# Second expert layers: one ScalarE function, h tanh(softplus(h)), used twice in place of sigmoid, square, reciprocal and products

## The chip, the core and the metric

The kernel runs on one core of a Trainium2 chip. The metric is device time in microseconds (us), the median of several executions. A core has five engines that run their own instruction queues in order and meet only through semaphores: TensorE (PE, with its weight loads shown as PEld), VectorE (DVE), ScalarE (ACT), GpSimd (POOL) and SyncE (SP), which issues the DMA transfers.

## What is computed

Attention over 4 batches, 8 heads and 576 tokens, in which only scores within tau of a row's maximum count, feeds two expert layers, each with 2304 tokens, width 512 and hidden width 2048. The change lies in the second:

```python
def _moe2_ref(x, w_in, w_out) -> np.ndarray:
    h = x @ w_in
    sp = np.where(h > 20.0, h, np.log1p(np.exp(np.minimum(h, 20.0))))
    g = h * np.tanh(sp)
    return (g @ w_out).astype(np.float32)
```

So between the two products of the second layer each element of h becomes g = h tanh(softplus(h)). With d = sigmoid(h) and t = (d - 1)^2 this is h (1 - t) / (1 + t), which is what the kernel before works out.

## The kernel before, in words

Every product is made from two-part operands: a value is split into a high part in TensorE's reduced 32-bit format (fp32r) and a low part, the rest. A product takes three terms: high by high, low by high and high by low.

The program has three stages: attention together with the first expert layer for the first three batches, the first layer for the last batch (while the weights of the second layer are split), and the second layer, `moe2`, which is the stage of this study. The weights arrive as `wraw`, are scaled by ACT (L64), put together in `wa` by DVE (L66 to L68, three instructions), and split into high part (ACT, L71) and low part (POOL, L72). The last quarters of the second product's weights, `w2o` in the rows, are still being split when `moe2` begins; the generator `rest` puts those steps between the stage's own.

`moe2` works on five blocks of tokens, four of 512 columns and one (number 4, the fourth in order) of 256. A block has 16 hidden chunks `fc` of 128 rows, 80 pairs (block, chunk) in all. For each pair:

- `hidden`: 12 matmuls make the chunk of h in PSUM. Even chunks use the pool `hp`, odd ones `mm` (named `hm`), with two buffers each, so chunk i + 4 needs the buffer of chunk i back.
- `act1`, `act2`, `act3` and `low`: the function. ACT makes the sigmoid d from h (L505) and the square t (L506). POOL makes -1 - t in d (L510). DVE makes (t - 1) h in t, which is the last reader of h (L511), and the reciprocal of d (L512). POOL multiplies t and d (L516), ACT copies the high part g2h (L519), POOL subtracts it to get the low part g2l (L523).
- `output`: 12 matmuls (6 in the block of 256 columns) add the chunk's part to the output sums o_0 to o_3, eight or four with g2h first, then those with g2l.

Code order is given by the loop at the end of `moe2`: in step i come `hidden` of chunk i, the functions, and `output` of chunk i - LAG, with LAG = 3. `act3` works on the chunk of the step before. The order of instructions in each engine's queue is then set by a scheduler, which may move them from code order. After chunk 15 the sums are copied to `os` by ACT (L548) and DVE (L546), and SP stores them (L552).

The tags `gh` and `gl` of the pool `gp` have six buffers each; d and g2h are allocated from the first, t and g2l from the second.

Of the kernel before, what the change touches and what calls it, by code (L numbers as in the profile page):

```python
# [8 lines left out]
F32 = mybir.dt.float32  # L9
F32R = mybir.dt.float32r  # L10
I32 = mybir.dt.int32
AF = mybir.ActivationFunctionType
ALU = mybir.AluOpType
PSUM = bass.MemoryType.PSUM

P = 128
# [3 lines left out]
class Fused:  # L20
# [12 lines left out]
    def consts(self, pool):  # L33
        nc = self.nc
        i2 = pool.tile([P, 192], F32, name="ident")
        self.ident, self.swap = i2[:, 0:128], i2[:, 64:192]
        make_identity(nc, self.ident)
        nc.gpsimd.tensor_copy(i2[:, 128:192], i2[:, 0:64])
        self.tau_c = pool.tile([P, 1], F32, name="tau_c")
        self.s_c = pool.tile([P, 1], F32, name="s_c")  # L40
        self.b_c = pool.tile([P, 1], F32, name="b_c")
        self.neg1 = pool.tile([P, 1], F32, name="neg1")
        nc.gpsimd.memset(self.neg1, -1.0)
        self.colsum = pool.tile([P, 4], F32, name="colsum")
        self.cb = pool.tile([P, 4], F32, name="cb")

# [279 lines left out]
    def attention(self):  # L326
# [4 lines left out]
        N = 9 * self.B * self.NP  # L331
        LAG = 7
        for n in "kq":
# [8 lines left out]
        tes = {}  # L342
        for k in range(N + LAG + 2):
            pr, ti = divmod(k, 9)
# [12 lines left out]
            elif fin:  # L357
                fin()
                fin = None
            j = k - LAG  # L360
            if 0 <= j < N:
# [109 lines left out]
    def moe2(self, rest):  # L471
        nc = self.nc
        blocks = (0, 1, 2, 4, 3)
        work = [(bi, fc) for bi in blocks for fc in range(16)]
        ys, hps, gs, outs = {}, {}, {}, {}

        def load(bi):
            n = 512 if bi < 4 else 256
            ys[bi] = [], [], n
            for e in range(4):  # L480
                for i, tag in enumerate(("xh", "xl")):
                    t = self.xp.tile([P, n], F32R, tag=tag, name=f"y2{bi}_{e}_{i}")
                    nc.sync.dma_start(t.bitcast(F32), self.yT[bi, e, i] if bi < 4 else self.yrem[e, i])
                    ys[bi][i].append(t)

        def hidden(bi, fc):
            yh, yl, n = ys[bi]
            w = self.w2["i", fc // 4]
            fs = slice((fc % 4) * 128, (fc % 4) * 128 + 128)
            hp = self.mm.tile([P, 512], F32, tag="mm", name=f"hm{bi}_{fc}") if fc % 2 else \  # L490
                self.hp.tile([P, 512], F32, tag="hp", name=f"hp{bi}_{fc}")
            i = 0
            for kc in range(4):
                for wl, yy in ((0, yh), (0, yl), (1, yh)):
                    nc.tensor.matmul(hp[:, :n], w[:, wl, kc, fs], yy[kc], start=(i == 0), stop=(i == 11))  # L495
                    i += 1
            hps[bi, fc] = hp[:, :n]

        def act1(bi, fc):

            h = hps.pop((bi, fc))
            n = ys[bi][2]
            d = self.gp.tile([P, n], F32, tag="gh", name=f"d{bi}_{fc}")
            t = self.gp.tile([P, n], F32, tag="gl", name=f"t{bi}_{fc}")
            nc.scalar.activation(d, h, AF.Sigmoid)  # L505
            nc.scalar.activation(t, d, AF.Square, bias=self.neg1)  # L506
            return h, d, t

        def act2(bi, fc, h, d, t):
            nc.gpsimd.tensor_scalar(d, t, -1.0, -1.0, op0=ALU.mult, op1=ALU.add)  # L510
            nc.vector.scalar_tensor_tensor(t, t, 1.0, h, op0=ALU.subtract, op1=ALU.mult)  # L511
            nc.vector.reciprocal(d, d)  # L512

        def act3(bi, fc, h, d, t):
            n = ys[bi][2]
            nc.gpsimd.tensor_tensor(t, t, d, op=ALU.mult)  # L516
            gh = self.gp.tile([P, n], F32R, tag="gh", name=f"g2h{bi}_{fc}")
            gl = self.gp.tile([P, n], F32R, tag="gl", name=f"g2l{bi}_{fc}")
            nc.scalar.copy(gh, t)  # L519
            gs[bi, fc] = (gh, gl)  # L520

            def low():
                nc.gpsimd.tensor_tensor(gl, t, gh.bitcast(F32), op=ALU.subtract)  # L523

            return low

        def output(bi, fc):
            gh, gl = gs.pop((bi, fc))
            n = ys[bi][2]
            w = self.w2["o", fc // 4]  # L530
            terms = [(gh, 0), (gh, 1), (gl, 0)]
            todo = [(i, t) for i in range(3) for t in range(n // 128)]
            if fc == 15:
                todo.sort(key=lambda it: it[1])
            for i, t in todo:
                if fc == 0 and i == 0:
                    outs[t] = self.op.tile([P, 512], F32, tag=f"o{t}", name=f"o{bi}_{t}")
                g, wl = terms[i]
                nc.tensor.matmul(outs[t], g[:, t * 128:t * 128 + 128], w[:, wl, fc % 4, :],  # L539
                                 start=(fc == 0 and i == 0), stop=(fc == 15 and i == 2))  # L540
            if fc < 15:
                return
            for t in range(n // 128):
                o = self.yp.tile([P, 512], F32, tag=f"y{t}", name=f"os{bi}_{t}")
                if t % 2:
                    nc.vector.tensor_copy(o, outs[t])  # L546
                else:
                    nc.scalar.copy(o, outs[t])  # L548
                if bi < 4:

                    dst = self.out[bi * 576:bi * 576 + 512, :].rearrange("(j c) e -> c j e", c=4)[t]
                    nc.sync.dma_start(dst, o)  # L552
                else:
                    for i in range(2):
                        r0 = (2 * t + i) * 576 + 512
                        nc.sync.dma_start(self.out[r0:r0 + 64, :], o[64 * i:64 * i + 64, :])

        LAG = 3
        load(0)
        prev = None  # L560
        n = len(work)
        for i in range(n + LAG):
            if i < n:
                bi, fc = work[i]
                if fc == 11 and bi != blocks[-1]:
                    load(blocks[blocks.index(bi) + 1])
                hidden(bi, fc)
                cur = (bi, fc) + act1(bi, fc)
            else:
                cur = None  # L570
            low = act3(*prev) if prev else None
            if cur:
                act2(*cur)
            if low:
                low()
            prev = cur
            if i >= LAG:
                output(*work[i - LAG])
            for _ in range(2):
                next(rest, None)  # L580
            yield 5200
# [136 lines left out]
```

## Time and profile before

| | |
|---|---|
| median of 3 runs | 1219.41 us (1215.17 to 1219.55) |
| the profiled execution | 1216.89 us |
| its span, first to last instruction | 1215.1 us |
| `moe2`, first matmul to last (start times of the trace) | 792.69 to 1208.46 us |
| busy over the span: PE, DVE, ACT, POOL | 95%, 71%, 49%, 54% |
| mean granted TensorE clock | 0.984 of full |

The profiled execution is 1.8 us longer than its span and lies 2.5 us under the median. Each engine's busy share is an average over stages that have different limits, so what follows is read from `moe2` alone. A matmul in the trace has a modelled end, after which the next has long begun: for the pace of TensorE the start times count, not the durations.

### The profile page before, as it was taken

The page shows a single profiled execution, that of the slowest core. Times are in us where ns is not written, and L with a number is a line of the kernel's source. Part 1 is how long each engine was busy: PE and PEld are TensorE (multiplying, and loading weights), DVE is VectorE, ACT ScalarE, POOL GpSimd, SP SyncE. Part 2 cuts the span into 40 slices and gives each one's busy share as a digit, 9 for nine tenths or more (in the row PEclk, how much of TensorE's full clock was granted, in tenths as well). Part 3 has the DMA queues.
Part 4 walks back from the last instruction along what each step waited for, and adds up shares of the span by engine and source line. Part 5 has one row for each costly group of instructions (what it writes and reads, how often), then busy time and mean ns, then how long its engine had stood idle before and what let it go on. Part 6 is the DMA issues. An engine that isn't in the chain of part 4 may idle for free.

```text
span 1215.1 us, 20290 instructions
## 1 busy us (share of the span) xinstructions
PE 1153.1 (95%) x7104; PEld 983.9 (81%) x7104; DVE 868.4 (71%) x1585; ACT 592.5 (49%) x1153; POOL 657.9 (54%) x841
## 2 busy tenths in 40 slices
PE   5888999999899999999999999988999999999998
PEld 4666878877788998988998999966888888888886
DVE  5888777878885465664652799799977676767865
ACT  4666666575555544455532575453433333344332
POOL 5566777786644343335431354346755655555654
PEclk8989999999999999999999999989999999999999
DMA  5556466576585445474433898842130020020000
GB/s 129 157 142 180 111 210 183 168 208 175 175 288 165 144 144 165 127 227 132 131 99 111 288 323 267 293 148 70 36 104 1 1 70 1 8 97 1 18 1 35
DMA packets 123671, 161.88 MB, mean 133 GB/s; under 512 B 57392, under 2 KB 78896, under 8 KB 123568
## 3 DMA queue, kind: packets, MB, share of 16 engines
q1 hardware_dynamic: 123568, 160.58, 43.2%
q8 instruction: 56, 0.92, 0.3%
q14 instruction: 47, 0.39, 0.1%
HBM read 107.48 MB, written 30.93 MB: 114 GB/s over the span
## 4 chain that ended last, share of the span: by engine, by line
PE 59%; DVE 13%; DMA 10%; POOL 6%; issue 5%; ACT 4%; SPq 2%; DVEq 0%; ACTq 0%; POOLq 0%
PE o L539 12%; PE h L405 11%; PE y L405 9%; PE pv L313 6%; PE hp L495 6%; PE hm L495 6%; PE S L254 5%; DMA wraw<-in_moe_w_in_dram 5%; PE T L291 4%; DMA wraw<-in_moe_w_out_dram 3%; DVE d L512 3%; POOL e L279 2%; DVE wa L67 2%; DVE wa L68 2%; DVE wa L66 2%
## 5 line engine op out<-in xcount | busy, mean ns | idle before, releaser
L512 DVE RECIPROCAL d<-d 128x512 f32<-128x512 f32 (+1 forms) x80 | 242.0, 3025 | 0.0
L405 PE MATMUL y<-gh,w 128*128 128x288 f32 x768 | 164.0, 299 | 2.7 <-DVE y L452 2.7
L405 PE MATMUL h<-xh,w 128*128 128x288 f32 x768 | 164.8, 300 | 1.3 <-DMA w<-w 1.0
L269 DVE SCALAR_TENSOR_TENSOR e<-ns,st,e 128x576 f32<-128x576 f32 x128 | 120.9, 948 | 45.5 <-ACT e L265 30.1
L260 POOL TENSOR_SCALAR st<-st,tau_c 128x1 f32<-128x1 f32 x144 | 60.9, 424 | 165.9 <-DVE ns L258 151.0
L539 PE MATMUL o<-w2o,g2h 128*128 128x512 f32 x576 | 149.7, 395 | 0.1
L258 DVE TENSOR_SCALAR_CACHE_REDUCE ns<-S 128x576 f32<-128x576 f32 x144 | 107.8, 752 | 55.6 <-PE S L254 54.9
L279 POOL TENSOR_SCALAR e<-e,st 128x576 f32<-128x576 f32 x128 | 126.4, 997 | 31.3 <-DVE st L274 28.9
L405 PEld LDWEIGHTS y<-gh,w 128*128 128x128 f32 x768 | 125.7, 188 | 10.2 <-issue 4.4
L265 ACT ACTIVATE e<-ns,st 128x576 f32<-128x576 f32 x128 | 98.9, 776 | 70.6 <-DVE ns L258 59.5
L405 PEld LDWEIGHTS h<-xh,w 128*128 128x128 f32 x768 | 125.7, 188 | 8.5 <-issue 5.7
L539 PEld LDWEIGHTS o<-w2o,g2h 128*128 128x128 f32 x576 | 107.1, 188 | 24.8 <-ACT g2h L519 0.6
L302 ACT COPY te<-T 128x576 f32<-128x576 f32 x144 | 91.3, 634 | 72.1 <-PE T L296 64.9
L429 POOL TENSOR_TENSOR gl<-rr,gh 128x288 fp32r<-128x288 f32 x96 | 81.0, 850 | 73.8 <-DVE rr L428 63.2
L495 PE MATMUL hp<-y,w2i 128*128 128x512 f32 (+1 forms) x480 | 113.6, 380 | 6.1 <-DVE t L511 6.0
L516 POOL TENSOR_TENSOR t<-t,d 128x512 f32<-128x512 f32 (+1 forms) x80 | 94.9, 1186 | 40.5 <-DVE d L512 40.3
L523 POOL TENSOR_TENSOR g2l<-t,g2h 128x512 fp32r<-128x512 f32 (+1 forms) x80 | 95.5, 1193 | 38.4 <-ACT g2h L519 36.1
L405 PE MATMUL y<-gl,w 128*128 128x288 f32 x384 | 113.7, 296 | 1.5 <-DVE gl L429 1.5
L405 PE MATMUL h<-xl,w 128*128 128x288 f32 x384 | 113.8, 296 | 0.0
L495 PE MATMUL hm<-y,w2i 128*128 128x512 f32 (+1 forms) x480 | 110.1, 373 | 3.1 <-DVE t L511 3.0
L254 PE MATMUL S<-KH,Q 128*128 128x288 f32 x320 | 101.6, 333 | 11.8 <-DVE ns L258 4.0
L291 PE MATMUL T<-ident,e 128*128 128x128 f32 x576 | 99.1, 281 | 13.6 <-ACT te L302 9.3
(100 smaller groups left out, 2481.8 us busy)
## 6 DMA issues: line engine op xcount, KB each, us to landing
w<-w SPq DMA_DIRECT2D x96, 512.0 KB, 4.2
wraw<-in_moe_w_in_dram SPq DMA_DIRECT2D x64, 256.0 KB, 3.9
w<-wp SPq DMA_DIRECT2D x32, 512.0 KB, 4.0
wraw<-in_moe_w_out_dram SPq DMA_DIRECT2D x64, 256.0 KB, 4.3
KH<-hik SPq DMA_DIRECT2D x60, 144.0 KB, 2.5
y<-yT SPq DMA_DIRECT2D x32, 256.0 KB, 4.1
KL<-lok SPq DMA_DIRECT2D x30, 144.0 KB, 2.7
rawq<-in_q_dram SPq DMA_DIRECT2D x32, 128.0 KB, 3.1
```

Source lines behind the costliest of these rows:

```text
L254: nc.tensor.matmul(so, Q[:, c0:c0 + 128], kt[:, ks], start=(i == 0), stop=(i == len(terms) - 1))
L258: nc.vector.tensor_scalar(ns.rearrange("p (h n) -> p h n", h=2), sv, -0.125, 3.0e38, op0=ALU.mult, op1=ALU.min, accum_out=nm[:, c1])
L265: nc.scalar.activation(e, ns, AF.Exp, bias=nm[:, c1], scale=-1.0)
L269: nc.vector.scalar_tensor_tensor(e, ns, nthr[:, c1], e, op0=ALU.is_le, op1=ALU.mult, accum_out=sm[:, c1])
L279: nc.gpsimd.tensor_scalar(t, t, rinv[:, j:j + 1], u[:, j:j + 1], op0=ALU.mult, op1=ALU.add)
L291: nc.tensor.transpose(T[:, i * 128:i * 128 + 128], self.es[pr, i, "pair"][:, o:o + 128], self.ident)
L405: nc.tensor.matmul(acc[:, :n], w[:, wl, c], rhs[c][xl][:, ts], start=(i == 0), stop=(i == 11))
L495: nc.tensor.matmul(hp[:, :n], w[:, wl, kc, fs], yy[kc], start=(i == 0), stop=(i == 11))
L512: nc.vector.reciprocal(d, d)
L516: nc.gpsimd.tensor_tensor(t, t, d, op=ALU.mult)
L523: nc.gpsimd.tensor_tensor(gl, t, gh.bitcast(F32), op=ALU.subtract)
L539: nc.tensor.matmul(outs[t], g[:, t * 128:t * 128 + 128], w[:, wl, fc % 4, :], start=(fc == 0 and i == 0), stop=(fc == 15 and i == 2))
```

## The change

ACT makes g from h in one instruction, with its own function for h tanh(softplus(h)) (called Mish in the code), and does so twice: once rounded into the high part g2h, once in full 32 bits into t. DVE subtracts the one from the other, which gives g2l. Both ACT instructions read h from PSUM, and the second is its last reader. POOL has no part in the function any more. LAG becomes 2, and the functions of a step are all issued in that step. The constant `neg1` is gone.

```diff
-        def act1(bi, fc):
+        def act(bi, fc):
...
             h = hps.pop((bi, fc))
             n = ys[bi][2]
-            d = self.gp.tile([P, n], F32, tag="gh", name=f"d{bi}_{fc}")
-            t = self.gp.tile([P, n], F32, tag="gl", name=f"t{bi}_{fc}")
-            nc.scalar.activation(d, h, AF.Sigmoid)
-            nc.scalar.activation(t, d, AF.Square, bias=self.neg1)
-            return h, d, t
-
-        def act2(bi, fc, h, d, t):
-            nc.gpsimd.tensor_scalar(d, t, -1.0, -1.0, op0=ALU.mult, op1=ALU.add)
-            nc.vector.scalar_tensor_tensor(t, t, 1.0, h, op0=ALU.subtract, op1=ALU.mult)
-            nc.vector.reciprocal(d, d)
-
-        def act3(bi, fc, h, d, t):
-            n = ys[bi][2]
-            nc.gpsimd.tensor_tensor(t, t, d, op=ALU.mult)
             gh = self.gp.tile([P, n], F32R, tag="gh", name=f"g2h{bi}_{fc}")
             gl = self.gp.tile([P, n], F32R, tag="gl", name=f"g2l{bi}_{fc}")
-            nc.scalar.copy(gh, t)
+            t = self.gp.tile([P, n], F32, tag="gl", name=f"t{bi}_{fc}")
+            nc.scalar.activation(gh, h, AF.Mish)
+            nc.scalar.activation(t, h, AF.Mish)
+            nc.vector.tensor_tensor(gl, t, gh.bitcast(F32), op=ALU.subtract)
             gs[bi, fc] = (gh, gl)
-
-            def low():
-                nc.gpsimd.tensor_tensor(gl, t, gh.bitcast(F32), op=ALU.subtract)
-
-            return low
...
-        LAG = 3
+        LAG = 2
```

The queues are the same up to the start of `moe2`, but for the constant. There they part. The first place is TensorE's queue (PE) where the third hidden chunk of block 0, hp_2, ends. Before, the next rows are those of the fourth chunk (hm_3), and chunks 4 and 5 follow before any output:

```order
L495 MATMUL hp_2_10281<-y_3_0_10208,w2i_8569 128x512
L495 MATMUL hm_3_10324<-y_0_0_10196,w2i_8569 128x512
L495 MATMUL hm_3_10324<-y_0_1_10198,w2i_8569 128x512
...
L495 MATMUL hm_5_10439<-y_3_0_10208,w2i_9012 128x512
L539 MATMUL o_0_10349<-w2o_8797,g2h_0_10258 128x512
L539 MATMUL o_1_10351<-w2o_8797,g2h_0_10258 128x512
```

In the changed kernel the rows at the same place are:

```order
L493 MATMUL hp_2_10272<-y_3_0_10206,w2i_8567 128x512
L522 MATMUL o_0_10291<-w2o_8795,g2h_0_10223 128x512
L522 MATMUL o_1_10293<-w2o_8795,g2h_0_10223 128x512
L522 MATMUL o_2_10295<-w2o_8795,g2h_0_10223 128x512
L522 MATMUL o_3_10297<-w2o_8795,g2h_0_10223 128x512
```

The output of chunk 0 has moved ahead of hidden chunks 3, 4 and 5; from there hidden and output take turns.

The second place is ACT's queue at the same time, with the scaling of weights (wraw) and their high parts (w2o) between the functions. Before:

```order
L505 ACT_TABLE_LOAD
L505 ACTIVATE d_0_10225<-hp_0_10212 128x512
L506 ACTIVATE t_0_10226<-d_0_10225,neg_77 128x512
L71 CAST w2o_10232<-wa_10314 128x256
L71 CAST w2o_10232<-wa_10323 128x256
L505 ACTIVATE d_1_10253<-hm_1_10240 128x512
L506 ACTIVATE t_1_10254<-d_1_10253,neg_77 128x512
L64 ACTIVATE wraw_10427<-wraw_10427 128x256
L64 ACTIVATE wraw_10436<-wraw_10436 128x256
L71 CAST w2o_10232<-wa_10373 128x256
L71 CAST w2o_10232<-wa_10382 128x256
L519 CAST g2h_0_10258<-t_0_10226 128x512
```

In the changed kernel:

```order
L505 ACT_TABLE_LOAD
L505 ACTIVATE g2h_0_10223<-hp_0_10210 128x512
L506 ACTIVATE t_0_10225<-hp_0_10210 128x512
L69 CAST w2o_10229<-wa_10315 128x256
L69 CAST w2o_10229<-wa_10324 128x256
L505 ACTIVATE g2h_1_10250<-hm_1_10237 128x512
L506 ACTIVATE t_1_10252<-hm_1_10237 128x512
L62 ACTIVATE wraw_10412<-wraw_10412 128x256
L69 CAST w2o_10229<-wa_10364 128x256
L69 CAST w2o_10229<-wa_10373 128x256
L62 ACTIVATE wraw_10421<-wraw_10421 128x256
L505 ACTIVATE g2h_2_10285<-hp_2_10272 128x512
```

The high part of chunk 0 now comes where its sigmoid was, eight rows earlier in the queue than its copy was; one table load stands in the stage in either kernel.

The third place is DVE's queue, where the first instruction on a chunk of h stands between the steps that put weights together (wa). Before:

```order
L68 SCALAR_TENSOR_TENSOR wa_10323<-wraw_10321,wa_10323 128x256
L67 SCALAR_TENSOR_TENSOR wa_10373<-wraw_10371,wa_10373 128x256
L67 SCALAR_TENSOR_TENSOR wa_10382<-wraw_10380,wa_10382 128x256
L511 SCALAR_TENSOR_TENSOR t_0_10226<-t_0_10226,hp_0_10212 128x512
L512 RECIPROCAL d_0_10225<-d_0_10225 128x512
```

In the changed kernel:

```order
L66 SCALAR_TENSOR_TENSOR wa_10324<-wraw_10322,wa_10324 128x256
L507 TENSOR_TENSOR g2l_0_10224<-t_0_10225,g2h_0_10223 128x512
L65 SCALAR_TENSOR_TENSOR wa_10364<-wraw_10362,wa_10364 128x256
L65 SCALAR_TENSOR_TENSOR wa_10373<-wraw_10371,wa_10373 128x256
L66 SCALAR_TENSOR_TENSOR wa_10364<-wraw_10362,wa_10364 128x256
L66 SCALAR_TENSOR_TENSOR wa_10373<-wraw_10371,wa_10373 128x256
L507 TENSOR_TENSOR g2l_1_10251<-t_1_10252,g2h_1_10250 128x512
```

The subtraction for chunk 0 stands two rows earlier than the product with h did, right behind the last step of wa_10324, and the reciprocals are gone.

## Rows read from the trace of the kernel before

**Rows 1.** Busy time in stretches: length; PE, PEld, DVE, ACT, POOL; clock, DMA share, GB/s.

```profile
800.00:860.00 60.00, 50.80 (x201) 38.54 (x200) 59.43 (x55) 26.85 (x52) 38.97 (x41) 0.94 0.30 87
860.00:1200.00 340.00, 340.00 (x1556) 278.77 (x1555) 251.24 (x148) 128.76 (x219) 203.19 (x213) 1.00 0.08 27
```

**Rows 2.** Waits of PE from 800 to 1216: us in total, times, longest.

```profile
PE hp L495 <- DVE t L511: 6.0, 3, 3.3
PE hm L495 <- DVE t L511: 3.0, 2, 1.5
```

**Rows 3.** Chain that ended last, steady part: start us, us, what.

```profile
912.66 2.77 PE o L539 x12
...
993.68 2.81 PE hm L495 x12
...
1066.33 1.41 PE hp L495 x12
```

**Rows 4.** Groups of instructions from 870 to 1206, by form: busy, mean ns, idle before.

```profile
L512 DVE RECIPROCAL d<-d 128x512 f32<-128x512 f32 x53 | 177.3, 3346 | 0.0
...
L516 POOL TENSOR_TENSOR t<-t,d 128x512 f32<-128x512 f32 x54 | 69.9, 1294 | 21.3 <-DVE d L512 21.1
...
L506 ACT ACTIVATE t<-d,neg 128x512 f32<-128x512 f32 x52 | 37.7, 725 | 1.6
...
L512 DVE RECIPROCAL d<-d 128x256 f32<-128x256 f32 x16 | 27.9, 1745 | 0.0
L511 DVE SCALAR_TENSOR_TENSOR t<-t,hm 128x512 f32<-128x512 f32 x26 | 17.9, 687 | 30.8 <-POOL d L510 30.7
...
L505 ACT ACTIVATE d<-hm 128x512 f32<-128x512 f32 x26 | 15.6, 598 | 62.5 <-PE hm L495 62.5
```

**Rows 5.** Timeline at the stage's start: start us, us, engine, line, what, idle before.

```profile
792.69 2.97 PE L495 MATMUL hp<-y,w2i 128*128 128x512 f32 x12
...
801.12 2.98 PE L495 MATMUL hm<-y,w2i 128*128 128x512 f32 x12
801.31 1.28 ACT L505 ACT_TABLE_LOAD   x1
...
802.60 0.60 ACT L505 ACTIVATE d<-hp 128x512 f32<-128x512 f32 x1
...
805.64 0.41 DVE L68 SCALAR_TENSOR_TENSOR wa<-wraw,wa 128x256 int32<-128x256 int32 x1
...
807.38 5.49 PE L495 MATMUL hp<-y,w2i 128*128 128x512 f32 x12 [3.28 <-DVE t L511]
...
809.09 0.44 ACT L64 ACTIVATE wraw<-wraw 128x256 f32<-128x256 f32 x1 [1.01 <-DMA wraw<-in_moe_w_out_dram]
...
814.41 2.60 PE L495 MATMUL hm<-y,w2i 128*128 128x512 f32 x10 [1.54 <-DVE t L511]
```

**Rows 6.** Stretches of 1 us, columns as in the first group.

```profile
275.00:276.00 1.00, 0.00 (x0) 0.00 (x0) 1.00 (x5) 1.00 (x3) 0.25 (x1) 1.00 0.04 16
278.00:279.00 1.00, 1.00 (x6) 1.00 (x6) 0.46 (x3) 0.83 (x2) 0.87 (x2) 0.50 0.00 0
807.00:808.00 1.00, 0.62 (x2) 0.53 (x3) 1.00 (x2) 0.98 (x2) 0.41 (x2) 0.50 0.70 145
```

**Rows 7.** Timeline at the end, columns as in the fifth group.

```profile
1200.62 2.02 PE L539 MATMUL o<-w2o,g2h 128*128 128x512 f32 x8
...
1203.41 2.02 PE L539 MATMUL o<-w2o,g2h 128*128 128x512 f32 x8
1204.50 1.29 POOL L516 TENSOR_TENSOR t<-t,d 128x512 f32<-128x512 f32 x1 [2.62 <-DVE d L512]
...
1206.49 2.13 PE L539 MATMUL o<-w2o,g2h 128*128 128x512 f32 x8
...
1208.46 1.08 PE L539 MATMUL o<-w2o,g2l 128*128 128x512 f32 x4
...
1209.51 1.80 SPq L552 DMA_DIRECT2D out_dram<-os  x4
```

More of the change, by code (lines that the diff above doesn't have):

```diff
@@ L41, in consts @@
         self.b_c = pool.tile([P, 1], F32, name="b_c")
-        self.neg1 = pool.tile([P, 1], F32, name="neg1")
-        nc.gpsimd.memset(self.neg1, -1.0)
         self.colsum = pool.tile([P, 4], F32, name="colsum")
@@ L556, in output @@
                         nc.sync.dma_start(self.out[r0:r0 + 64, :], o[64 * i:64 * i + 64, :])
-        LAG = 3
+        LAG = 2
         load(0)
-        prev = None
         n = len(work)
@@ L567, in moe2 @@
                 hidden(bi, fc)
[L568 to L576, printed above, removed]
+                act(bi, fc)
             if i >= LAG:
```

## The prediction, made before the changed kernel ran

> **What bounds the kernel now.** Only `moe2` changes, so I first cut its time into stretches. From 860 to 1200 us PE is busy for 340.00 of 340 us at full clock; from 800 to 860 it is busy for 50.80 of 60 only, while DVE is busy for 59.43 [rows 1]. The waits of PE put those gaps down to one thing: 3 + 2 waits, 9.0 us together, for DVE's L511, the product with h that gives a PSUM buffer back [rows 2]. So the stage has a short start in which PE waits for DVE, and a long steady part in which it waits for nobody.
>
> How much could be won at all? I take PE's pace from start times. From 912.66 to 993.68 there are 29 groups of 12 matmuls: 81.02 / 348 = 0.2328 us each; a group with 256 columns takes 1.41 us [rows 3]. Four blocks have 64 x 24 matmuls of 512 columns, 357.6 us; block 4 has 16 x (1.41 + 6 x 0.2328) = 44.9 us; together 402.5. The stage's matmuls go from 792.69 [rows 5] to 1208.46 + 4 x 0.2328 = 1209.39 [rows 7], 416.7 us. **14.2 us** are lost, and no change of the functions can win more unless it changes PE's pace.
>
> Where are they? At the end, the last group starts at 1206.49 where 1203.41 + 12 x 0.2328 = 1206.20 would have been possible: 0.3, and some 0.1 for starting again [rows 7]. The rest, 13.8, is lost at the start. Its largest wait is that of hp_4, at 807.38 instead of 801.12 + 2.79 = 803.91: 3.5 us. The clock then stands at half: the 12 matmuls of hp_4 span 5.49 us, 2.3 to 2.7 too much [rows 5, 6].
>
> **In the steady part the change is worth nothing.** Per chunk, DVE loses the 3.35 us reciprocal and 0.69 for L511, and gains one subtraction. POOL loses all its work, of which the product alone is 1.29. ACT loses three instructions and has two new ones [rows 4]. All of it lies beside 24 x 0.2328 = 5.59 us of PE work. The cover for the new chain is wide: between the end of hidden(i) and output(i) PE now has output(i-2), hidden(i+1), output(i-1) and hidden(i+2), 11.2 us, or 5.6 in block 4, for a chain of about 2 us. Without that cover each chunk would pay those 2 us.
>
> **Prices of the new instructions.** Mish doesn't occur in the trace. The nearest row is the sigmoid, same engine, same PSUM source, same size: 0.598 us; the square, with its bias column, took 0.725 [rows 4]. I take 0.60, bounds 0.60 and 0.73; a third, far bound, the reciprocal's 3.35, is a rival below. DVE's subtraction of 128x512: the nearest row is L511 of the same size, 0.69, which I take; the bounds are 0.60, ACT's for one operand, and 1.29, POOL's product of two operands [rows 4].
>
> **The start, step by step.** PE now meets the output of chunk 0 before hm_3, so it has to wait where it didn't.
> - PE ends hp_2 and is free at 801.12 [rows 5].
> - ACT reaches chunk 0 after its table load: 801.31 + 1.28 = 802.60, as before, since nothing ahead of it changes [rows 5]. g2h_0 is there at 803.20, t_0 at 803.80. PE begins o(0) at 803.25: **a wait of 2.1 us.** Eight matmuls take it to 805.1.
> - g2l_0 stands on DVE behind the step of wa that ends at 805.64 + 0.41 = 806.05 [rows 5]. With 0.69 it is there at 806.75: **a wait of 1.6 us.** Four matmuls, then hm_3 from 807.7 to 810.5.
> - o(1) at 810.5: ACT has one cast left that needs the same step of wa, then g2h_1 at 807.1 and t_1 at 807.7. DVE has four steps of about 0.41 and g2l_1 at 809.1, needed at 812.4. Covered by 3.3 us.
> - o(2) at 816.1: on ACT, g2h_2 waits behind the scale whose DMA let it start at 809.09 [rows 5], so 810.1. Covered by 6 us.
> - o(3) at 821.7: nine weight instructions of some 0.43 stand ahead of g2h_3, 3.9 us of work and some waiting for DMAs that DVE's steps set free; even doubled, it is there by 819. From there PE doesn't wait.
> - Hidden chunks: hp_4 needs t_0 done, 803.8, long past. The wait that cost 3.5 us, and its four successors, have no cause left.
>
> Waits 3.7, and 0.1 each for starting again: 3.9 us.
>
> **The clock.** After the wait for hp_4 it was at 0.50 [rows 6]. It also fell near 277, where PE had been idle from 275 to 276 and a little around it; by 278 it was at 0.50 [rows 6]. But the wait of 1.54 us that ended at 814.41 [rows 5] was followed by full speed. Two waits of 2.1 and 1.6 us, so close together, lie between; I think a fall likelier than not. If it comes behind the first, o(0) runs at half speed, its first eight matmuls end near 806.9 instead of 805.1, and the second wait is gone: of the 2.7 us of the fall, 1.3 were lost anyway. I charge **1.4 us**; bounds 0 (no fall) and 3.4 (a later, longer fall that hides nothing).
>
> **The sum.** Lost before 14.2; lost after 3.9 + 1.4 = 5.3; saved 8.9. At the end, the high part of chunk 15 is there long before 1206.20 (already in the 14.2). What follows the last matmul gets shorter too: the last group's output now finishes o_0 and o_1 early, so SP's four stores, which before began at 1209.51 and stood in line for 1.80 us [rows 7], begin earlier and only the last waits for its copy: about 0.5 saved. Together **9.4 us**: 1216.89 - 9.4 = 1207.5 on the profiled execution, 1210.0 counted from the median, which lies 2.5 above it. I give **1208.5**.
>
> **Rivals.**
> 1. *The loss comes back as another wait.* ACT's queue is in order, and a late weight DMA holds up g2h_1 to g2h_4 behind it. For: a scale waited 1.01 us there [rows 5]. Against: covers of 3.3 to 6 us. If it brought back half of the saving, the time would be about 1213; if PE's low clock lasted too, 1215.
> 2. *The table load is not one but many.* If Mish and the plain copies didn't share a table, each turn between them on ACT would cost the 1.28 us of [rows 5]: some 8 turns up to g2h_4, 10 us, of which the covers take 5 or 6. That gives about 1213. Against: both queues show one load. The Trainium skill, "ScalarE: Activation LUTs", section "Table sets: the hidden batching unit", says that sets must be switched between functions of different sets, which speaks against a new function, and that cheap functions stand in every set, which speaks for one load; the trace, with sigmoid, square and copies behind one load, agrees with the latter.
> 3. *Slower: Mish is a long instruction.* The place is ACT in the steady part, and the point is 5.59 / 2 = 2.8 us each, 4.7 times the sigmoid. As long as the reciprocal it would make a chunk 2 x 3.35 = 6.69 us instead of 5.59, and 2 x 1.745 = 3.49 instead of 2.81 in block 4 [rows 4]: 64 x 1.10 + 16 x 0.68 = 81 us, so about 1290. Nothing in the trace speaks for it; Mish is unseen, no more.
> 4. *PE's pace itself improves*, because POOL and DVE leave the memory alone. If 0.2328 became 512 columns at 2.4 GHz, 0.2133, 64 x 24 x 0.0195 = 30 us and block 4's share, 4, would come on top, about 1174. Against: from 1200.62 to 1203.41, 12 matmuls took 2.79 as ever, though POOL rested for the 2.62 us before 1204.50 [rows 7]. The Trainium skill, "TensorE: Matmul & The Clock Gate", section "Wait — 56ns, not 53.3ns?", states 0.2157 for 512 columns once warm, in bf16; by that the sum would be 64 x 24 x 0.0171 = 26 us lower. The trace doesn't agree, whatever POOL did.
>
> **Chances and range.** Forecast 0.82, rival 1 0.11, rival 2 0.02, rival 3 0.03, rival 4 0.02. The forecast's own range: without a fall of the clock 1.4 less, with the long one 2.0 more, the bounds of the two new instructions 0.1 less to 0.8 more; around 1207.5 to 1210.0 that makes 1206 to 1213. With half of rival 1 and the runs' own spread (1215.17 to 1219.55) I give 1204 to 1214. A measurement of this kernel can tell about 0.5%, 6.1 us, from no change: faster means below 1213.3. The forecast holds that in 19 of 20 cases, rival 4 always, rival 1 rarely: faster 0.80, same 0.16, slower 0.04.
>
> **What would show it.** Right: in the new profile PE has two waits near 801 and 805, for ACT's g2h_0 and DVE's g2l_0, of about 2.1 and 1.6 us, and none after 810; groups of 12 still start 2.79 us apart; Mish reads 0.60; one table load; POOL has nothing after the weights; the last output starts with no gap. Wrong: waits for ACT between 810 and 830, a second stretch at half clock, loads between functions, or another pace in the steady part.

## The result, and the profile after

| | before | changed |
|---|---|---|
| median | 1219.48 us (4 runs, 1215.17 to 1222.22) | 1204.92 us (4 runs, 1204.01 to 1208.18) |
| the profiled execution, and its span | 1216.89, 1215.08 us | 1204.01, 1201.85 us |
| `moe2`, first matmul to start of the last | 416.46 us | 404.63 us |
| start of the last matmul to the end of the span | 5.93 us | 5.00 us |

The changed kernel takes 0.9894 of the time before (95% interval 0.9866 to 0.9922). That is 14.6 us less between the medians and 13.2 us less between the two profiled spans; the forecast was 1208.5 us, with a range from 1204 to 1214. Of the 13.2 us, `moe2` gives 11.8 and the stretch behind its last matmul 0.9; the stage also begins 0.5 us earlier, at 792.22, though nothing ahead of it but a constant changed.

The page of the changed kernel first: busy time, share of the span and instructions of each engine.

```profile
PE 1145.2 (95%) x7104; PEld 979.2 (81%) x7104; DVE 626.1 (52%) x1505; ACT 529.7 (44%) x1073; POOL 427.3 (36%) x600
```

DVE falls from 71% to 52% and POOL from 54% to 36%, yet PE's share stays at 95%. As before, the page says little about where the time went. The view by stretches of the changed kernel, columns as in [rows 1], does:

```profile
800.00:860.00 60.00, 57.76 (x248) 46.01 (x247) 25.48 (x49) 22.51 (x48) 15.91 (x15) 1.00 0.27 84
860.00:1180.00 320.00, 320.00 (x1473) 262.64 (x1472) 45.98 (x73) 68.11 (x139) 0.00 (x0) 1.00 0.09 29
```

In the first 60 us PE's busy time rose from 50.80 to 57.76, and the clock from 0.94 to 1.00. In the steady part PE was busy all the time before, and is so now; DVE, at 74% of [rows 1], is down to 14%, and POOL does nothing at all. That relief bought no time: the chain of work that ended last, in the steady part of the changed kernel (start us, us, what), goes at the old pace.

```profile
901.30 2.80 PE hp L493 x12
...
1046.64 2.80 PE hp L493 x12
```

Between these two rows lie 52 groups of 12 matmuls: 145.34 / 624 = 0.2329 us each, against 0.2328 in [rows 3].

The waits of PE in the changed kernel, from 792 to 1215 (us in total, times, longest), in place of the five of [rows 2]:

```profile
PE o L522 <- ACT g2h L505: 1.9, 1, 1.9
PE o L522 <- DVE g2l L507: 0.4, 1, 0.4
```

And the timeline where they stand, columns as in [rows 5]:

```profile
797.81 2.96 PE L493 MATMUL hp<-y,w2i 128*128 128x512 f32 x12
...
800.69 1.28 ACT L505 ACT_TABLE_LOAD   x1
801.99 0.60 ACT L505 ACTIVATE g2h<-hp 128x512 fp32r<-128x512 f32 x1
802.48 0.59 ACT L506 ACTIVATE t<-hp 128x512 f32<-128x512 f32 x1
802.64 2.12 PE L522 MATMUL o<-w2o,g2h 128*128 128x512 f32 x8 [1.86 <-ACT g2h L505]
803.66 0.48 DVE L64 TENSOR_SCALAR wa<-wraw 128x256 int32<-128x256 int32 x2
804.40 0.68 DVE L507 TENSOR_TENSOR g2l<-t,g2h 128x512 fp32r<-128x512 f32 x1
805.13 1.19 PE L522 MATMUL o<-w2o,g2l 128*128 128x512 f32 x4 [0.37 <-DVE g2l L507]
806.16 2.96 PE L493 MATMUL hm<-y,w2i 128*128 128x512 f32 x12
```

The reader sees the forecast's step: the high part of chunk 0, which by the rows of the two queues has moved up by ten places in ACT's queue, not eight, comes right behind the table load; output of chunk 0 follows hp_2, waits for the table load and one Mish, then shortly for the subtraction, and from 806 hidden and output take turns. The 5.49 us of hp_4 at half clock [rows 5, 6] have no counterpart.

The groups of the new instructions, from 870 to 1190, by form (columns as in [rows 4]):

```profile
L507 DVE TENSOR_TENSOR g2l<-t,g2h 128x512 fp32r<-128x512 f32 x49 | 33.9, 692 | 232.4 <-ACT t L506 232.4
...
L505 ACT ACTIVATE g2h<-hm 128x512 fp32r<-128x512 f32 x25 | 14.9, 598 | 111.2 <-PE hm L493 111.2
L506 ACT ACTIVATE t<-hm 128x512 f32<-128x512 f32 x25 | 14.8, 593 | 0.0
```

Mish reads 598 and 593 ns where the sigmoid read 598, and DVE's subtraction 692 where L511 read 687. ACT stands idle before these rows because it waits for PE's hidden chunk, and DVE because it waits for ACT: it is PE that now sets the pace from the first chunks on.

### The profile page after: what moved, and what is told of

It reads as the page before. It is cut to its first block, busy times and chain, and to the rows that moved or that the text cites. A ratio compares the mean times of both kernels' runs of the same rounds, so it can differ in the third digit from the quotient of the medians.

```text
span 1201.8 us, 19799 instructions
## 1 busy us (share of the span) xinstructions
PE 1145.2 (95%) x7104; PEld 979.2 (81%) x7104; DVE 626.1 (52%) x1505; ACT 529.7 (44%) x1073; POOL 427.3 (36%) x600
## 4 chain that ended last, share of the span: by engine, by line
PE 69%; DMA 10%; DVE 8%; POOL 5%; issue 3%; ACT 2%; SPq 2%; DVEq 0%; ACTq 0%; POOLq 0%
PE o L522 17%; PE h L403 11%; PE y L403 10%; PE hm L493 8%; PE hp L493 8%; PE pv L311 6%; DMA wraw<-in_moe_w_in_dram 4%; PE S L252 4%; DMA wraw<-in_moe_w_out_dram 4%; PE T L289 3%; POOL e L277 3%; DVE wa L64 1%; DMA w<-w 1%; DVE wa L65 1%; DVE wa L66 1%
## 5 line engine op out<-in xcount | busy, mean ns | idle before, releaser
L507 DVE TENSOR_TENSOR g2l<-t,g2h 128x512 fp32r<-128x512 f32 (+1 forms) x80 | 51.9, 648 | 315.4 <-ACT t L506 311.6
L403 PEld LDWEIGHTS y<-gh,w 128*128 128x128 f32 x768 | 125.8, 188 | 11.1 <-issue 4.4
L252 PE MATMUL S<-KH,Q 128*128 128x288 f32 x320 | 100.3, 329 | 14.6 <-DVE ns L256 5.0
L493 PE MATMUL hp<-y,w2i 128*128 128x512 f32 (+1 forms) x480 | 107.2, 372 | 0.0
L311 PE MATMUL pv<-te,rawv 128*64 128x288 f32 x640 | 105.6, 420 | 0.0
L493 PEld LDWEIGHTS hm<-y,w2i 128*128 128x128 f32 x480 | 84.5, 188 | 18.0
```

The source lines that it names most:

```text
L252: nc.tensor.matmul(so, Q[:, c0:c0 + 128], kt[:, ks], start=(i == 0), stop=(i == len(terms) - 1))
L311: self.nc.tensor.matmul(self.pv[HALVES[h], hf * HB:hf * HB + 288], v[:, h, c, :], tes[h][:, hf * 288:hf * 288 + 288], start=first, stop=last)
L403: nc.tensor.matmul(acc[:, :n], w[:, wl, c], rhs[c][xl][:, ts], start=(i == 0), stop=(i == 11))
```

## The experiments

All but e2_first12 and e3_rest start from the changed kernel. The stage is timed from its first matmul's start to its last's; the last column is its excess over e1_lag3, in which no wait of PE was left. In e5 to e8, e10 and e11 the added instructions make values that nothing reads. Where an expectation names a theory by a letter, A is the account of the prediction (the gain lies at the stage's start, the steady part gives nothing), and the others are what the expectation says of them; in e5_dve_load and e6_pool_load theory A says in addition what that engine's load should do. e5 to e11 ran once each, so a difference of 1 us between two of them can be a single fall of the clock (told below).

| kernel | us | runs | stage | excess |
|---|---|---|---|---|
| before | 1219.48 | 4 | 416.46 | 14.7 |
| changed | 1204.92 | 4 | 404.63 | 2.9 |
| e12_after_again | 1205.51 | 5 | 404.46 | 2.7 |
| e1_lag3 | 1201.90 | 4 | 401.75 | 0 |
| e13_lag3_again | 1201.65 | 4 | 401.78 | 0.0 |
| e2_first12 | 1205.43 | 4 | 403.55 | 1.8 |
| e3_rest | 1215.80 | 10 | 416.02 | 14.3 |
| e9_unsorted | 1205.73 | 1 | 404.93 | 3.2 |
| e5_dve_load | 1204.50 | 1 | 405.62 | 3.9 |
| e6_pool_load | 1211.62 | 1 | 408.83 | 7.1 |
| e7_act4 | 1202.72 | 1 | 405.72 | 4.0 |
| e8_act8 | 1211.69 | 1 | 407.04 | 5.3 |
| e10_both | 1212.49 | 1 | 410.81 | 9.1 |
| e11_release | 1204.07 | 1 | 407.54 | 5.8 |

The kernel before took 1216.2 us beside e1, e2, e3 and e9 (13 runs), 1217.76 beside e5 to e8 (1 run) and 1218.45 beside e10 to e13 (9 runs).

**Where in the stage does the gain lie?** e2_first12 uses the new function in the first 12 chunks only, e3_rest in the other 68 only. Both are made from the kernel before, with its LAG = 3; `mish` is the function `act` of the changed kernel.

```diff
-                cur = (bi, fc) + act1(bi, fc)
+                cur = None
+                if i < 12:        # e3_rest: i >= 12
+                    mish(bi, fc)
+                else:
+                    cur = (bi, fc) + act1(bi, fc)
```

> The kernel before, LAG = 3, with the new function for the first 12 chunks of block 0 alone and the old functions for the other 68. Theory A (the whole gain of the change lies at the start of the stage, where DVE has the last weights to put together as well): the stage takes 402 to 404 us, plus up to 1 for the old end, so as fast as the changed kernel or faster. Rival B (the gain lies in the long part, by a better pace of PE once POOL and DVE rest): the stage takes 412 us or more, most of the 416.5 of before.

> The reverse: the old functions for the first 12 chunks, the new one for the other 68. Theory A: the waits of PE from 804 to 848 and the fall of the clock come back, the stage takes 415 to 417 us as before (the gap of 0.4 at the end is gone) and the whole is within 0.3% of before. Rival B: the stage takes 406 us or less.

e2_first12 took 0.9907 (0.988 to 0.9934) of the time before, e3_rest 0.999 (0.9975 to 1.0004). In e2_first12 the stretches and PE's one wait read:

```profile
800.00:860.00 60.00, 59.87 (x257) 47.98 (x256) 27.43 (x52) 25.23 (x52) 14.74 (x17) 1.00 0.27 89
860.00:1180.00 320.00, 320.00 (x1470) 262.59 (x1469) 232.90 (x138) 119.28 (x203) 185.31 (x195) 1.00 0.09 29
...
PE o L550 <- ACT g2h L530: 0.3, 1, 0.3
```

and in e3_rest the first stretch and the waits:

```profile
800.00:860.00 60.00, 50.21 (x202) 38.77 (x201) 59.73 (x56) 26.13 (x50) 38.97 (x42) 0.94 0.26 82
...
PE hp L495 <- DVE t L522: 5.8, 3, 3.2
PE hm L495 <- DVE t L522: 3.9, 1, 3.9
```

Twelve of 80 chunks bring the stage to 403.55 us, less than the changed kernel's 404.63, with DVE as busy as ever (232.90 of 320 us) in the steady part; the other 68 bring it from 416.46 to 416.02, and leave waits of 9.7 us and the 0.94 of the clock. So the gain in the stage comes from its start, but for some 0.4 us, and LAG = 2 isn't its cause, since e2_first12 has 3.

**What does LAG = 2 cost?** e1_lag3, and once more e13_lag3_again beside e12_after_again, the changed kernel itself:

```diff
-        LAG = 2
+        LAG = 3
```

> The changed kernel with LAG = 3: hidden chunk 3 stands ahead of the output of chunk 0 again, nothing else differs. Theory A (the loss that is left at the start is PE waiting for g2h_0 and g2l_0 of chunk 0, 1.9 and 0.4 us): 2.8 us of hidden work cover both waits, so PE shows no wait from 792 to the end and the stage, first hidden matmul to last output matmul, takes 404.6 - 2.5 = 402.1 us; about 1202.5 us in all. Rival C (the shorter lag is what brought the gain): the waits for buffers come back, the stage takes 410 us or more.

> The changed kernel with LAG = 3 again, on the same chip. Theory A: no wait of PE in the stage, 401.8 us, and 2 to 4 us less than the changed kernel in all (2.8 us of waits, and about 1 more in executions in which the clock falls); ratio to before 0.986.

> The changed kernel again, beside the next one on the same chip. All theories: about 0.989 of before, the stage 404 to 406 us, depending on whether the clock falls in the wait of 2 us at its start.

e1_lag3 took 0.9882 of the time before (0.9867 to 0.9898); e13_lag3_again 0.9871 (0.9846 to 0.9896), on the chip on which the changed kernel took 0.9896 (0.9877 to 0.9916). The first stretch of e13_lag3_again:

```profile
800.00:860.00 60.00, 60.00 (x259) 48.42 (x258) 25.41 (x50) 23.22 (x49) 15.12 (x14) 1.00 0.26 81
```

PE is busy for 60.00 of 60 us: with one more hidden chunk ahead of the first output, the table load and Mish are covered, and both waits are gone. The stage is 2.7 to 2.9 us shorter, the medians 3.9 us on the same chip (1205.51 to 1201.65). This is the fastest version here; the intervals of the two ratios overlap, but each version's two stages agree within 0.2 us.

**What shortened the stretch behind the last matmul?** e9_unsorted takes the sort out of the last chunk's output:

```diff
-            if fc == 15:
-                todo.sort(key=lambda it: it[1])
```

> The changed kernel without the order by output tile in the last chunk of each block, so that the four sums end together. Theory A's last term (what follows the last matmul got 1.0 us shorter because o_0 and o_1 end early): from the start of the last matmul to the end of the span 5.9 us as before, instead of 4.95; the rest of the stage unchanged, 404.6 us. Rival (the end got shorter for another reason, such as DVE and ACT being free): 4.95 stays.

The end in the changed kernel, timeline columns as in [rows 7]:

```profile
1195.65 0.58 ACT L531 COPY os<-o 128x512 f32<-128x512 f32 x1 [5.66 <-PE o L522]
1196.26 2.06 SPq L535 DMA_DIRECT2D out_dram<-os  x4
...
1196.85 0.39 PE L522 MATMUL o<-w2o,g2l 128*128 128x512 f32 x1
1197.27 0.69 DVE L529 COPY os<-o 128x512 f32<-128x512 f32 x1 [0.70 <-PE o L522]
```

and in e9_unsorted:

```profile
1196.97 1.10 PE L520 MATMUL o<-w2o,g2l 128*128 128x512 f32 x4
1197.63 1.29 DVE L527 COPY os<-o 128x512 f32<-128x512 f32 x2 [6.10 <-PE o L520]
1198.01 1.80 SPq L533 DMA_DIRECT2D out_dram<-os  x4
```

With the sort SP's four stores begin before the last matmul; without it they begin after it and stand in line for 1.80 us, as in [rows 7]. From the last matmul's start to the end it is 5.92 us, where the kernel before has 5.93 and the changed one 5.00 (the 4.95 of the expectation came from a rounded span). So the order by output tile is worth the 0.9 us. The sort stands in the code of the kernel before too, but there the last chunk's matmuls ran eight with g2h and then four with g2l all the same [rows 7]. Where the new function makes the last chunk they run tile by tile: this stretch is 4.54 us in e3_rest, and 6.15 in e2_first12, whose last chunk has the old functions.

**Was it the load on DVE and POOL?** In the kernel before, PE waits for DVE's L511, and DVE is full. Either DVE and POOL had too much to do, or the chain from h to L511 was long. e5_dve_load and e6_pool_load give about the old work back to one engine each, off the chain; e10_both to both; e11_release also returns h's buffer late, behind DVE's reciprocal.

```diff
             nc.vector.tensor_tensor(gl, t, gh.bitcast(F32), op=ALU.subtract)
+            nc.vector.reciprocal(t, t)                        # e5, e10, e11
+            nc.vector.tensor_copy(t, h)                       # e11
+            for _ in range(2):                                # e6; e10 with gh, gh
+                nc.gpsimd.tensor_tensor(t, t, gh.bitcast(F32), op=ALU.mult)
```

> The changed kernel with one reciprocal on DVE behind each subtraction, on a tile that nobody reads any more: DVE's load per chunk is that of before again (about 4.0 us), the chain from h to g2l is as short as in the changed kernel. It gives results that aren't used. Theory A (at the start it is DVE's load that makes PE wait): waits of PE for g2l between 810 and 850, the stage takes 410 to 416 us; the long part keeps its pace of 0.233 us per matmul. Rival D (it was the long chain over three engines, not DVE's load): the stage takes 406 us or less.

> The changed kernel with two products of 128x512 on GpSimd behind each subtraction, on a tile that nobody reads any more, so that GpSimd has 2.6 us per chunk again. Theory A: GpSimd's load costs DVE some sharing at the start only, the second wait grows from 0.4 to at most 1.6 us, the stage takes 404.6 to 407 us. Rival E (GpSimd's load is what slowed DVE at the start): waits between 810 and 850, the stage takes 409 us or more.

> The changed kernel with both loads off the chain: a reciprocal on DVE and two products on GpSimd per chunk, on a tile that nobody reads. DVE's load alone gave no wait. Theory F (before, DVE fell behind at the start because its weight steps, slowed by GpSimd's work, and the reciprocals together are more than PE's 5.59 us per chunk, whatever the chain): PE waits for g2l between 810 and 850, the stage takes 410 to 416 us. Theory D (the loads don't matter off the chain; what cost the time was the long chain that every chunk had to pass before its output and its buffer): the stage takes 404 to 409 us.

> The changed kernel in which DVE reads h last, as before: behind the subtraction a reciprocal and a copy of h from PSUM, both into a tile that nobody reads. So the buffer of a hidden chunk comes free late, but its output is ready early. Theory G (the late return of the PSUM buffers alone made PE wait): waits of hidden matmuls for DVE return, the stage takes 410 us or more. Theory D (the long chain to the output was needed as well, since PE had no output work to do meanwhile): PE has outputs to do, the stage takes 404 to 408 us.

The first stretch of e5_dve_load, its one wait of PE, and its timeline behind it:

```profile
800.00:860.00 60.00, 58.00 (x243) 46.34 (x243) 59.83 (x61) 22.37 (x47) 13.05 (x15) 0.97 0.27 85
...
PE o L523 <- ACT g2h L505: 2.0, 1, 2.0
...
802.69 3.44 PE L523 MATMUL o<-w2o,g2h 128*128 128x512 f32 x8 [2.00 <-ACT g2h L505]
...
805.92 1.38 PE L523 MATMUL o<-w2o,g2l 128*128 128x512 f32 x4
```

DVE is busy for 59.83 of 60 us, more than before the change, and PE doesn't wait for it once. The stage, 405.62 us, is where rival D has it and not theory A: a full DVE by itself doesn't make the loss. The excess over the changed kernel, 1.0 us, is one fall of the clock (told below).

The waits of PE in e6_pool_load:

```profile
PE o L524 <- ACT g2h L505: 3.9, 3, 1.9
PE o L524 <- DVE g2l L507: 0.4, 1, 0.4
```

Its new loss is a second wait for ACT's g2h, of 1.80 us, and a fall of the clock behind it (0.50 from 826.4). ACT was held in its queue by a cast of weights that waited for DVE's L66 (timeline):

```profile
824.65 0.40 ACT L69 CAST w2o<-wa 128x256 fp32r<-128x256 f32 x1 [1.97 <-DVE wa L66]
...
825.93 3.40 PE L524 MATMUL o<-w2o,g2h 128*128 128x512 f32 x8 [1.80 <-ACT g2h L505]
```

That is a wait in ACT's queue, as in the prediction's first rival, but a DVE step beside POOL's products held it up, not a DMA. The stage, 408.83 us, lies above the 407 of theory A and just under the 409 of rival E: POOL's load does cost time here. The first stretch of e10_both, and its waits:

```profile
800.00:860.00 60.00, 55.11 (x220) 42.88 (x220) 58.51 (x57) 22.86 (x49) 32.30 (x32) 0.94 0.32 100
...
PE o L525 <- DVE g2l L507: 2.9, 2, 2.2
PE o L525 <- ACT g2h L505: 1.8, 1, 1.8
```

With both loads, waits of output for DVE return, and the clock's 0.94; the excess is 9.1 us, some way towards the 14.7 of before, though ACT gives h's buffer back early. That is theory F's figure (410.81 us of 410 to 416). In e11_release, a late return with DVE's load alone, the waits are

```profile
PE o L524 <- ACT g2h L505: 2.0, 1, 2.0
PE o L524 <- DVE g2l L507: 1.4, 2, 0.8
```

and no hidden matmul waits for a buffer: the scheduler puts outputs ahead of the hidden chunks there, so PE's order isn't that of the kernel before, and the run doesn't settle what a late return costs in the old order.

What the two loads do to each other is in the groups of DVE, from 800 to 860, by form: the last of the three steps that put weights together. In the changed kernel:

```profile
L66 DVE SCALAR_TENSOR_TENSOR wa<-wraw,wa 128x256 int32<-128x256 int32 x12 | 5.2, 448 | 0.1
```

In e5_dve_load:

```profile
L66 DVE SCALAR_TENSOR_TENSOR wa<-wraw,wa 128x256 int32<-128x256 int32 x12 | 4.4, 404 | 0.0
```

In e6_pool_load:

```profile
L66 DVE SCALAR_TENSOR_TENSOR wa<-wraw,wa 128x256 int32<-128x256 int32 x12 | 6.9, 577 | 0.1
```

In e10_both:

```profile
L66 DVE SCALAR_TENSOR_TENSOR wa<-wraw,wa 128x256 int32<-128x256 int32 x12 | 8.7, 754 | 0.0
```

In the kernel before the same step (L68 there) took 845 ns. All 36 steps of the three lines together took 26.2 us before, 17.7 in the changed kernel, 14.9, 25.2 and 22.8 in e5, e6 and e10. These steps are longer in the kernels in which POOL has products beside them, and not in the one in which DVE alone got more to do. The Trainium skill, "SBUF — State Buffer", section "SBUF: two separate sides", says that DVE and GpSimd share a pair of ports as an exclusive lock, which an instruction of DVE with two SBUF inputs takes against a GpSimd instruction that reads SBUF. These rows agree with it: both inputs of L66 lie in SBUF, and it goes from 448 to 577 and 754 ns beside POOL's products.

The trace of the kernel before says more on what PE waited for there. POOL's L510 is the last step that L511 has to wait for, since it reads t before L511 writes over it; these are its rows and L511's (timeline), for chunks 0 and 1 and then L511 for chunk 6, with a pair of weight steps:

```profile
804.13 0.73 POOL L510 TENSOR_SCALAR d<-t 128x512 f32<-128x512 f32 x1 [1.30 <-ACT t L506]
...
804.29 1.43 DVE L66 TENSOR_SCALAR wa<-wraw 128x256 int32<-128x256 int32 x2
...
806.65 0.67 DVE L511 SCALAR_TENSOR_TENSOR t<-t,hp 128x512 f32<-128x512 f32 x1
...
807.91 0.62 POOL L510 TENSOR_SCALAR d<-t 128x512 f32<-128x512 f32 x1 [0.59 <-ACT t L506]
...
813.68 0.68 DVE L511 SCALAR_TENSOR_TENSOR t<-t,hm 128x512 f32<-128x512 f32 x1
...
847.32 0.67 DVE L511 SCALAR_TENSOR_TENSOR t<-t,hp 128x512 f32<-128x512 f32 x1
```

In the first wait, that of hp_4, the chain was late by about 1 us (L510 ended at 804.86, PE was free at 803.91), and weight steps kept DVE until 806.65. In the other four, L510 had ended more than 5 us before DVE came to L511, and DVE was busy for 44.00 of the 44 us from 804 to 848. From chunk 0 to chunk 6 its L511s lie (847.32 - 806.65) / 6 = 6.78 us apart, where PE has 5.59 us of work per chunk. So what PE waited for was mostly DVE's full queue, with the release of h in it, and only in the first wait the chain as well.

**How long may the function on ACT be?** e7_act4 and e8_act8 add four and eight uses of Mish to each chunk.

```diff
             nc.vector.tensor_tensor(gl, t, gh.bitcast(F32), op=ALU.subtract)
+            for _ in range(4):        # e8_act8: 8
+                nc.scalar.activation(t, t, AF.Mish)
```

> The changed kernel with four more uses of the new function per chunk on ScalarE, on a tile that nobody reads any more, about 0.6 us each. Theory A: in the long part ScalarE has some 3.6 of 5.59 us, PE doesn't wait, the pace stays; at the start ScalarE's queue gets longer by 2.4 us per chunk, which costs 0 to 5 us: the stage takes 405 to 410 us. Rival (the new function is near to being the bound): more than 420 us.

> The same with eight more: ScalarE has about 0.5 + 9 x 0.62 = 6.1 us per chunk of 512 columns and some 4.1 per chunk of 256, more than PE's 5.59 and 2.8. Theory A (the bound moves to ScalarE where two uses together pass 5.59 us): PE waits for ScalarE in every chunk, the stage takes 64 x 6.1 + 16 x 4.1 = 456 us, between 440 and 475. Rival (ScalarE overlaps its instructions so far that even ten fit): below 420 us.

The steady stretch of e7_act4:

```profile
860.00:1180.00 320.00, 320.00 (x1473) 262.46 (x1472) 45.31 (x73) 217.06 (x400) 0.00 (x0) 1.00 0.09 29
```

and of e8_act8, with the end of its timeline:

```profile
860.00:1180.00 320.00, 319.03 (x1467) 260.82 (x1466) 45.59 (x72) 308.27 (x658) 0.00 (x0) 1.00 0.09 29
...
1200.01 9.08 ACT L509 ACTIVATE t<-t 128x512 f32<-128x512 f32 x17
```

e7_act4 shows three times the ACT work hidden whole. e8_act8 is a miss: ten uses of some 0.6 us were expected to exceed the 5.59 us of a chunk and to make the stage some 456 us long; it took 407.04, with two waits of hidden matmuls for ACT of 0.5 us each. The last row tells why: 17 uses in 9.08 us are one every 0.53 us, though each reads 0.63 on average. In a row they overlap a little, and ten fit into 5.59 us. ACT is then the last to finish: the tail is 11.1 us, which is most of that kernel's loss.

## Why the prediction was right, step by step

- **The steady part gives nothing:** shown, by the pace (0.2329) and by e3_rest, whose 0.999 holds the new function in 68 chunks. PE's pace didn't improve without DVE and POOL beside it (rival 4).
- **The loss at the start goes:** shown, by e2_first12. By the prediction's count the stage now loses 404.63 + 0.23 - 402.5 = 2.4 us, not 5.3. The saving is 11.8 where 8.9 was forecast. The count's floor of 402.5 is itself 0.5 too high: e1_lag3, in which PE doesn't wait, takes 401.75 + 0.23 = 402.0, so that more than 14.2 us could be won.
- **The first wait** reads 1.9 us. The profile counts it from the modelled end of the matmul before; by start times, as the prediction counted, it is 802.64 - (797.81 + 2.79) = 2.0, forecast 2.1.
- **The second wait** reads 0.4, by start times 805.13 - (802.64 + 1.86) = 0.6, forecast 1.6. This is a mis-sized term. The working took DVE's rows up to the step of wa that ended at 806.05 as unchanged. But POOL's L510 had run beside the first of a pair of weight steps (L66 before, L64 now), and is gone: the pair that took 1.43 us took 0.48, which is the 1.0 us. A removed instruction can count on the engine beside it too. That L510 is the reason is argued from where the rows stand: no run isolates it, and a weight step of POOL (L72) ran beside the second of the pair. e6_pool_load shows POOL's products beside longer steps of this kind.
- **The clock** was charged 1.4 us for a fall that didn't come in the changed kernel's profile, nor in those of e12 and e9. In e6 it didn't come behind this wait either. It did come behind the same wait in e5 (the granted clock reads 0.50 from 803.1), e7 (801.0), e8 (802.4), e10 (806.3) and e11 (800.5). Where it came in e5, the price was of the kind forecast: eight matmuls of o(0) took 3.44 us instead of 2.12, the second wait vanished behind them, and the stage was 1.0 us longer than the changed kernel's. So the term was one of two outcomes, and what decides between them stays open: the waits were of 1.7 to 2.2 us in the kernels without the fall, and of 1.8 to 2.0 in those with it.
- **The tail** gave 0.9 us, forecast 0.5, by the mechanism named (e9_unsorted).
- **Together:** in the stage 0.1 and 1.0 from the two waits, 0.1 that was charged for starting again, 1.4 from the clock and 0.3 from the floor that was too high; then 0.4 in the tail and 0.5 by the earlier start. They make the 3.8 us between the forecast's 9.4 and the span's 13.2. All but the start err in one direction, with the saving set too low, and so 1204.92 us lies only 0.9 above the lower end of the range; the earlier start, which nothing in the change explains, is luck.
- **Rivals:** one table load of 1.28 us stands in the stage (rival 2 falls); Mish reads 0.60, and even ten uses per chunk keep PE busy for 319.03 of 320 us (rival 3 falls; its point was 2.8 us each); PE waits nowhere between 810 and 830 (rival 1 falls here; e6_pool_load shows a wait in ACT's queue once POOL is loaded, for DVE and not for a DMA).
- **Left open:** how much of the loss before each part of the old arrangement cost. The trace of before puts four of its five waits on DVE's full queue and not on the chain ahead of L511. DVE's load alone, with h's release moved to ACT, gives no wait of PE for DVE; both loads give 9.1 of 14.7 us. Whether the rest comes from h's release standing in that queue or from the old order of PE, in which no output stood ready to fill the gap, no run separates: e11_release met another order, and no run has both loads with the late release and LAG = 3. Where the 0.5 us of earlier start came from is open too: in these kernels, equal up to the stage but for a constant, it began anywhere from 789.75 to 796.02.

## What to carry to other kernels

Before pricing a cheaper function, split its stage into the stretch where the bound engine waits and the stretch where it doesn't: here 12 chunks of 80 held nearly all there was to win, and in the rest PE, busy all the time, hid the relief of three engines. When a change takes an engine's work away, reprice the neighbours that ran beside it, not only that engine. After such a change look again at the order: a lag that the shorter chain seemed to allow cost 2.7 to 2.9 us of the stage, and the old lag with the new function was fastest.

## What the runs showed that was not expected

- Ten uses of Mish per chunk fit in 5.59 us: in a row they start 0.53 us apart, while each reads 0.63.
- The same wait of about 2 us is followed by half clock in five kernels and by full clock in four, with PE's work ahead of it unchanged.
- The start of `moe2` moved by up to 6 us between kernels that are alike up to there, so a change inside a stage is better read from the stage's own length (404.63 and 404.46 in two runs) than from whole times (1203.63 to 1207.42 in five executions of one kernel).
